# Taking the first three weight pairs of unit 0 in two chunks of 128 tokens, with a new stored order

## The chip, the cores and the metric

The kernel runs on one core of a Trainium2 chip. The metric is device microseconds of one execution. Five engines of the core work side by side, each through its own queue in order: TensorE (PE) with its weight loads (PEld), VectorE (DVE), ScalarE (ACT), GpSimd (POOL), and SyncE (SP), which issues all DMAs here.

## What is computed

A gated linear attention (complex decays, 4 x 8 heads of 48, 768 tokens) whose output goes through a feed-forward layer of 384 x 2048 x 384. All is float32; the weights w_in and w_out come in as 64-bit floats. Cut to what matters:

```python
def _attn_ref(q, k, v, a_re, a_im):
    mag = np.sqrt(a_re * a_re + a_im * a_im)
    scale = np.minimum(mag, 0.999) / (mag + 1e-06)
    a_re_n, a_im_n = (a_re * scale, a_im * scale)
    ...
    for t in range(S):
        ar, ai = (a_re_n[:, :, t, :, None], a_im_n[:, :, t, :, None])
        new_re = ar * S_re - ai * S_im
        new_im = ar * S_im + ai * S_re
        kv = np.einsum('bhd,bhe->bhde', k[:, :, t], v[:, :, t])
        S_re, S_im = (new_re + kv, new_im)
        y[:, :, t] = np.einsum('bhd,bhde->bhe', q[:, :, t], S_re)
    return y

def _moe_ref(x, w_in, w_out):
    h = x @ w_in
    g = h * (1.0 / (1.0 + np.exp(-1.702 * h)))
    return g @ w_out
```

## The kernel before

The 3072 tokens are 12 units of 256 (`T`), three to a batch; a unit is two chunks of 128 (`L`). For each unit the kernel does three things.

`prepare` turns the decays of a unit into magnitudes and angles: squares, logarithms, exponentials and an arctangent on ACT, sums and scans along time on DVE, then cosines and sines, and q and k are scaled and rotated (`rot0`, `rot1`). The small correction of the reference (the 1e-6) is two activations in stage `logc`: an exponential, then a logarithm. ACT must load another function table whenever it goes between logarithms, trigonometry and the Silu of the feed-forward layer (line 837). `remap` then copies the rotated q and k from tile `qr` or `qk` into tile `qkh` by five DMAs each. Unit 0 alone is prepared in its two chunks, so that chunk 0 is ready first.

`attend` works chunk by chunk on PE: scores (line 499, named P below), a masked copy `pm` on DVE, transposed keys (line 555, K) with a copy `kt`, the state (line 549, Z), and the mix of both (line 524) into `x_ps`. An x copy on ACT (line 534) puts the 128 columns of a chunk into tile `x`.

`moe` runs the feed-forward layer for a block of units: units 0 and 1 alone, then two at a time. It goes through 8 weight pairs `A0`..`A7`, `U0`..`U7` (`NP`). A pair has two halves `f`; each half has an H piece (line 605: three matmuls by an A tile into `h_ps`), a Silu on ACT (line 614 for units 0 and 1) and an O piece (line 638: three matmuls by a U tile, added up in `o_ps`). Blocks 0 and 1 take the weights whole as float32; all later blocks take each product as three terms, of high and low halves. Before block 0 can use a pair, `convert` makes it from the raw 64-bit words: two integer operations and an add on DVE (lines 297, 301, 304), one activation on ACT (line 300), in buffers that are loaded again once they are free. Thirteen matmuls by the identity (`WARM`, line 446) stand ahead of the attention of unit 0 and write nothing that is used.

At the end, `decide` sees whether the data are in the range that this way of computing needs. For this `prepare` and `extent` (line 692) reduce the decays; the last `LATE` units do it where the decays lie already, the others are loaded again for it.

The order of all this isn't found by a scheduler at run time. Each step is recorded with its engine and what it reads and writes (`Plan.add`), and a stored table, `ORDER`, says in which order the steps are written out; `OTHER` names the steps that go to their second engine (ACT or DVE). Each engine runs its steps in that order and waits for others where data ask for it. The two lines that the order hangs on:

```python
    order = plan.order()
    ...
            if o[5] not in (None, cur):
                nc.scalar.preload_act_table_set(o[5])
```

Of the kernel before, what the change touches and what calls it, by code (L numbers as in the profile page):

```python
# [23 lines left out]
P = 128  # L24
# [21 lines left out]
A_MIN = 1e-20  # L46
LOG_MAX = math.log(0.999)
LIFT = 14.0
LATE = 3
# [20 lines left out]
class Plan:  # L70
# [90 lines left out]
def attention_moe(ctx: ExitStack, tc: tile.TileContext, qk_in, v, a_in, w_in, w_out, qn, kn, vn, an, bn, out):  # L161
# [7 lines left out]

    ident = sb.tile([P, P], F32, name="ident")  # L170
    mask = sb.tile([P, NQ, P], F32, name="mask")
    small = sb.tile([P, 4 + 2 * NR], F32, name="small")
    ones, b_tiny, b_hpi, good = (small[:, n : n + 1] for n in range(4))
    crs = [small[:, 4 + n * NR : 4 + (n + 1) * NR] for n in range(2)]
    n_a, n_w = (NU + 1) * NR, 2 * NP * WC // CK
# [836 lines left out]
```

## Time and profile before

| | us |
|---|---|
| median of 3 runs | 561.31 (560.44 to 562.53) |
| the profiled execution | 560.85 |
| its span, first to last instruction | 559.1 |
| PE busy in the span | 532.4 |
| DVE busy | 406.7 |
| ACT busy | 354.3, of which 94.9 in 74 table loads |
| first attention matmul, first MoE matmul | 25.36, 38.52 |

The span is what the rows below are counted in, from its start. A busy time is the union of an engine's instructions; ends of matmuls are modelled, so the step from one start to the next says more than a duration. The first column of a row of a timeline is the start.

### The profile page before, as it was taken

Reading aid. Unit: us, or ns where it says so; the run is one execution under the profiler, and the core shown is the slowest. Engines: PE = TensorE matmul, PEld = TensorE weight load, DVE = VectorE, ACT = ScalarE, POOL = GpSimd, SP = SyncE. Lnnn points to the kernel's source line nnn. Section 1 sums busy time; section 2 is a strip of 40 time slices with the busy share of each in tenths; the row PEclk is TensorE's granted clock in tenths of the full one; section 3 lists DMA queues with packets and bytes.
Section 4 is the critical chain, followed back from the end, with each engine's and each line's share of the span. In section 5 each row is a group of like instructions: output and inputs, shape, how many; then the busy total and the mean of one; then the engine's idle time right before and its main releaser. Section 6 shows DMA issues by size and latency. Waiting matters only on the chain.

```text
span 559.1 us, 14720 instructions
## 1 busy us (share of the span) xinstructions
PE 532.4 (95%) x6236; PEld 442.7 (79%) x6236; DVE 406.7 (73%) x733; ACT 354.3 (63%) x500; POOL 28.7 (5%) x86
## 2 busy tenths in 40 slices
PE   0599999999999999999999999999999999999996
PEld 0478888888888888888888888887888888888884
DVE  7999999999998898978958856686665444422132
ACT  8999999998997788688494746536362122122222
POOL 4300010101000000000000000000000000000000
PEclk9999999999999999999999999999999999999999
DMA  8679977683758677486556456538225331001101
GB/s 338 201 270 349 252 241 151 191 199 90 212 121 232 143 181 173 135 219 143 182 134 130 131 118 146 175 108 164 72 84 162 86 73 52 2 9 31 55 1 59
DMA packets 32341, 81.24 MB, mean 145 GB/s; under 512 B 4368, under 2 KB 8464, under 8 KB 32272
## 3 DMA queue, kind: packets, MB, share of 16 engines
q1 hardware_dynamic: 32272, 80.27, 52.9%
q8 instruction: 49, 0.80, 0.6%
q14 instruction: 20, 0.16, 0.1%
HBM read 56.62 MB, written 4.72 MB: 110 GB/s over the span
## 4 chain that ended last, share of the span: by engine, by line
PE 89%; ACT 4%; DVE 4%; issue 1%; DMA 1%; POOL 0%; DVEq 0%; ACTq 0%
PE o_ps L638 35%; PE h_ps L605 35%; PE x_ps L524 7%; PE p_ps L499 5%; PE kz_ps L555 4%; PE kz_ps L549 3%; DVE qk L277 1%; ACT L837 1%; ACT valA L300 1%; DVE qr L277 1%; DMA ri<-in_a_dram 1%; DVE valA L304 0%; DVE s L277 0%; DVE s L419 0%; ACT s L375 0%
## 5 line engine op out<-in xcount | busy, mean ns | idle before, releaser
L618 ACT ACTIVATE g<-h_ps 128x512 f32<-128x512 f32 x80 | 46.8, 595 | 100.2 <-PE h_ps L605 85.7
L837 ACT ACT_TABLE_LOAD x74 | 94.9, 1283 | 2.1 <-PEq L1000 0.8
L638 PE MATMUL o_ps<-gh,hiU 128*128 128x512 f32 x240 | 95.8, 399 | 0.0
L605 PE MATMUL h_ps<-xhi,hiA 128*128 128x512 f32 x240 | 95.4, 397 | 0.1
L638 PE MATMUL o_ps<-gl,hiU 128*128 128x512 f32 x240 | 93.8, 391 | 0.0
L605 PE MATMUL h_ps<-xhi,loA 128*128 128x512 f32 x240 | 93.7, 390 | 0.0
L638 PE MATMUL o_ps<-gh,loU 128*128 128x512 f32 x240 | 93.5, 390 | 0.0
L605 PE MATMUL h_ps<-xlo,hiA 128*128 128x512 f32 x240 | 93.5, 390 | 0.0
L624 DVE TENSOR_TENSOR gl<-g,gh 128x512 fp32r<-128x512 f32 x80 | 54.7, 688 | 47.5 <-ACT gh L621 45.6
L638 PEld LDWEIGHTS o_ps<-gl,hiU 128*128 128x128 f32 x240 | 45.0, 188 | 10.1 <-DVE gl L624 0.4
L605 PEld LDWEIGHTS h_ps<-xhi,loA 128*128 128x128 f32 x240 | 45.1, 188 | 9.6
L605 PEld LDWEIGHTS h_ps<-xlo,hiA 128*128 128x128 f32 x240 | 45.1, 188 | 9.0 <-issue 0.3
L638 PEld LDWEIGHTS o_ps<-gh,hiU 128*128 128x128 f32 x240 | 45.1, 188 | 9.0 <-issue 0.2
L605 PEld LDWEIGHTS h_ps<-xhi,hiA 128*128 128x128 f32 x240 | 45.1, 188 | 8.9 <-ACT g L618 0.2
L638 PEld LDWEIGHTS o_ps<-gh,loU 128*128 128x128 f32 x240 | 45.2, 188 | 8.6
L672 DVE TENSOR_REDUCE fit<-raw_w 128x1 f32<-128x256 f32 x96 | 36.6, 413 | 17.2 <-DMA raw_w<-in_w_out_dram 12.9
L638 PE MATMUL o_ps<-g,valU 128*128 128x256 f32 x192 | 46.2, 384 | 0.1
L277 DVE TENSOR_TENSOR qk<-qk,s 128x768 f32<-128x768 f32 (+1 forms) x52 | 45.6, 889 | 0.3
L605 PE MATMUL h_ps<-x,valA 128*128 128x256 f32 x192 | 45.3, 383 | 0.0
L621 ACT ACTIVATE gh<-g 128x512 fp32r<-128x512 f32 x40 | 25.0, 627 | 24.8 <-PE o_ps L638 24.1
L605 PEld LDWEIGHTS h_ps<-x,valA 128*128 128x128 f32 x192 | 35.7, 190 | 5.2 <-ACT g L614 0.4
L638 PEld LDWEIGHTS o_ps<-g,valU 128*128 128x128 f32 x192 | 35.5, 190 | 5.5 <-ACT g L614 0.5
(96 smaller groups left out, 824.9 us busy)
## 6 DMA issues: line engine op xcount, KB each, us to landing
v<-in_v_dram SPq DMA_DIRECT2D x24, 416.0 KB, 4.5
ri<-in_a_dram SPq DMA_DIRECT2D x11, 768.0 KB, 5.4
qk<-in_qk_dram SPq DMA_DIRECT2D x11, 768.0 KB, 5.7
qkh<-qr SPq DMA_DIRECT2D x22, 288.6 KB, 6.0
qkh<-qk SPq DMA_DIRECT2D x22, 288.6 KB, 5.9
raw<-in_w_in_dram SPq DMA_DIRECT2D x8, 768.0 KB, 6.1
raw<-in_w_out_dram SPq DMA_DIRECT2D x8, 768.0 KB, 6.6
raw_w<-in_w_in_dram SPq DMA_DIRECT2D x24, 256.0 KB, 2.9
```

The source lines that it names most:

```text
L277: add(en, t, rank, lambda: e.tensor_tensor(out=out, in0=a, in1=b, op=alu), **kw)
L499: mm(p_ps[to : to + QL, j, lo:L], lhsT=at(h, 1, c)[:, lo : lo + QL], rhs=at(h, 0, c)[:, lo:L], start=True, stop=True)
L524: mm(x_ps[32 * j : 32 * j + 32, r, :], lhsT=lt, rhs=rt, start=n == 0, stop=n == len(steps) - 1)
L549: mm(z_ps[a:b, j * VP + lo : j * VP + lo + D], lhsT=kt[0][:, j, a:b], rhs=vt[:, h * VP + lo : h * VP + lo + D], start=True, stop=True)
L555: nc.tensor.transpose(k_ps[:, j, :], at(4 * hh + 2 * e + j, 1, c)[0:KD], ident[0:KD, 0:KD])
L605: mm(h_ps[hb][:, hs], lhsT=ww[:, r * T + f * P : r * T + (f + 1) * P], rhs=x[:, r, :], start=r + k == 0, stop=r == NR - 1 and k == len(ter ...
L618: add("ACT", a_t(N) - 0.15, rk(i + f / 2), lambda hb=hb, hs=hs: act(out=g32[hb][:, hs], in_=h_ps[hb][:, hs], func=AF.Silu, scale=SLOPE), r ...
L621: one = ("ACT", a_t(N) - 0.1, lambda hb=hb, hs=hs: act(out=high.g(hb)[:, hs], in_=g32[hb][:, hs], func=AF.Copy))
L624: add("DVE", d_t(N), rk(i + f / 2), lambda hb=hb, hs=hs: dve.tensor_tensor(out=glo[hb][:, hs], in0=g32[hb][:, hs], in1=high.g(hb)[:, hs].b ...
L638: mm(o_ps[m][:, 0:N], lhsT=y[:, f * DM + m * P : f * DM + (m + 1) * P], rhs=x[:, hs], start=i == 0 and f == 0 and k == 0, stop=i == NP - 1 ...
L672: add("DVE", d_t(CK), rk + 2, lambda x=x, op=op: dve.tensor_reduce(out=f_w[:, x, n : n + 1], in_=weights.looked_at()[:, :, 1], op=op, axis ...
L837: nc.scalar.preload_act_table_set(o[5])
```

## The change

Block 0 gets a list of steps in place of the loop over pairs: pairs 0, 1 and 2 (`EARLY = 3`) on chunk 0, the same three on chunk 1, then pairs 3 to 7 on all 256 columns. An H piece of a chunk reads that chunk's x copy alone; its matmuls have 128 columns. Besides:

- Stage `logc` is one exponential with a bias of log 1e-6 in place of an exponential and a logarithm.
- The first load of the decays, of chunk 0, is two DMAs, real parts first.
- The absolute value on DVE is a bitwise operation on integers.
- The range of the decays is judged by their real parts alone, against 0.125; `LATE` is 6, and `extent` loads real parts only, in two pieces a unit.
- In the last pair of the last block the three groups of half 0 stand ahead of those of half 1, and the last of three outputs is evicted and stored in two halves.
- `ORDER` and `OTHER` are new throughout.

In the whole program PE gets 36 matmuls more (72 of 128 columns for 36 of 256), ACT has 50 table loads in place of 79 and DVE 20 reductions fewer, among others. The counts include the fallback path that isn't run.

```diff
+EPS = 1e-6
+R_MIN = 0.125
-LATE = 3
+LATE = 6
+EARLY = 3
...
-        add("SP", z, rk("load"), lambda: dma(out=ri[:, cols], in_=a_in[u, :, cols]), w=ks("re", "im"))
+        for x in range(2) if u == i == 0 else (2,):
+            part = slice(cols.start + x % 2 * C, cols.stop if x else cols.start + C)
+            add("SP", z * (0.5 if x < 2 else 1), rk("load"), lambda part=part: dma(out=ri[:, part], in_=a_in[u, :, part]),
+                w=[k for n, kind in enumerate(("re", "im")) if x in (n, 2) for k in ks(kind)])
...
-        add("ACT", a_t(C) - 0.1, rk("logc"), lambda: act(out=c, in_=m, func=AF.Exp, scale=-0.5), r=k_mag, w=k_rec, tab=LOGS, grp=u or None)
-        add("ACT", a_t(C), rk("logc"), lambda: act(out=c, in_=c, func=AF.Ln, scale=1e-6, bias=ones), w=k_rec, tab=LOGS, grp=u or None)
+        add("ACT", a_t(C) - 0.1, rk("logc"), lambda: act(out=c, in_=m, func=AF.Exp, scale=-0.5, bias=b_eps), r=k_mag, w=k_rec, tab=LOGS, grp=u or None)
...
-        two = ("DVE", d_t(C), lambda: dve.scalar_tensor_tensor(out=cs, in0=t, scalar=-1.0, in1=t, op0=ALU.mult, op1=ALU.max))
+        two = ("DVE", w_t(C), lambda: dve.tensor_scalar(
+            out=cs.bitcast(I32), in0=t.bitcast(I32), scalar1=0x7FFFFFFF, scalar2=None, op0=ALU.bitwise_and,
+        ))
...
-        for i in range(NP):
-            def at(f, i=i):
-                k = (2 * i + f) % 2 if len(units) == 2 else 2 * f + i % 2
-                return k * N // (2 * T), slice(k * N % (2 * T), k * N % (2 * T) + N), f"{k * N // T}"
+        steps = [(i, 0, N) for i in range(NP)]
+        if n == 0:
+            steps = [(i, c * L, L) for c in range(2) for i in range(EARLY)] + steps[EARLY:]
+        for t, (i, c0, M) in enumerate(steps):
+            def at(f, i=i, t=t, M=M):
+                k = (2 * i + f) % 2 if len(units) == 2 else 2 * f + t % 2
+                return k * N // (2 * T), slice(k * N % (2 * T), k * N % (2 * T) + M), f"{k * N // T}"
+
+            nm = f"{n}c" if M < N else f"{n}"
+            xk = [f"x{y}{b}.{c}" for y in ("h" if whole else "hl") for c in range(c0 // L, (c0 + M) // L)]
...
-                        terms = [(weights.whole("A", i), high.x0(n))]
+                        terms = [(weights.whole("A", i), high.x0(n)[:, :, c0 : c0 + M])]
...
-                parts = [((0, 1), (m,)) for m in range(NR)]
+                parts = [((0,), tuple(range(NR)))] + [((1,), (m,)) for m in range(NR)]
...
+        pieces = [(m, 0, N) for m in range(NR)]
+        if final:
+            pieces[-1:] = [(NR - 1, 0, N // 2), (NR - 1, N // 2, N)]
```

Where the work of unit 0 stands on PE. In the kernel before, the last warm-up and the last K turn of chunk 1 stand ahead of the first H pieces (`x` is the tile of both chunks, `valA` an A tile, `h_ps` and `o_ps` the sums):

```order
L446 MATMUL h_ps_105<-qk,ident 128x256
L555 MATMUL kz_ps<-ident,qkh_75 128x112 x2
L605 MATMUL h_ps_106<-x_407,valA_157 128x256 x3
L605 MATMUL h_ps_105<-x_407,valA_293 128x256 x3
L605 MATMUL h_ps_106<-x_407,valA_293 128x256 x3
L605 MATMUL h_ps_105<-x_407,valA_157 128x256 x3
L638 MATMUL o_ps_107<-g_497,valU_181 128x256
```

In the changed kernel (its line 614 is line 605 of before, 503 is 499, 559 is 555), from the second H piece on:

```order
L614 MATMUL h_ps_105<-x_377,valA_215 128x128 x3
L503 MATMUL p_ps<-qkh_75 32x128 x4
L503 MATMUL p_ps<-qkh_75 32x96 x4
L503 MATMUL p_ps<-qkh_75 32x64 x4
L503 MATMUL p_ps<-qkh_75 32x32 x4
L559 MATMUL kz_ps<-ident,qkh_75 128x112 x2
L614 MATMUL h_ps_105<-x_377,valA_236 128x128 x3
L614 MATMUL h_ps_106<-x_377,valA_236 128x128 x3
L503 MATMUL p_ps<-qkh_75 32x128 x4
```

H pieces of 128 columns have moved between the scores of chunk 1; before, all scores came first.

On ACT, the kernel before has the two x copies (line 534) of unit 0 five rows apart, then a table load and the first Silu (line 614):

```order
L534 ACTIVATE x_407<-x_ps 128x3x128
L374 ACTIVATE s_81<-s_81 128x3x256
L558 ACTIVATE kt_97<-kz_ps 128x224
L837 ACT_TABLE_LOAD
L391 ACTIVATE s_81<-s_81 128x3x256
L534 ACTIVATE x_407<-x_ps 128x3x128
L300 ACTIVATE valA_467<-raw_72 128x768
L837 ACT_TABLE_LOAD
L614 ACTIVATE g_488<-h_ps_106 128x256
```

The changed kernel, from its first x copy (line 538) on; 623 is the Silu, 844 the table load, 303 a weight, and the others are steps of unit 1:

```order
L538 ACTIVATE x_377<-x_ps 128x3x128
L562 ACTIVATE kt_97<-kz_ps 128x224
L303 ACTIVATE valU_374<-raw_73 128x768
L428 ACTIVATE s_81<-s_85 128x3x256
L404 ACTIVATE s_80<-s_84 128x3x256
L405 ACTIVATE s_84<-s_84 128x771
L844 ACT_TABLE_LOAD
L623 ACTIVATE g_463<-h_ps_105 128x128
```

Its second x copy stands 19 rows behind the first:

```order
L844 ACT_TABLE_LOAD
L379 ACTIVATE s_81<-ri,small 128x3x256
L538 ACTIVATE x_377<-x_ps 128x3x128
L380 ACTIVATE s_81<-s_81 128x3x256
L381 ACTIVATE s_83<-s_83,small 128x3x256
L562 ACTIVATE kt_97<-kz_ps 128x224
L386 ACTIVATE s_84<-s_83,small 128x3x256
L844 ACT_TABLE_LOAD
L623 ACTIVATE g_463<-h_ps_105 128x128
```

Silus of chunk 0 now stand between the two x copies, and so do steps of unit 1 and 2 that came later before.

## Rows read from the trace of the kernel before

**Rows 1.** Page, part 1: busy us, share of the span, instructions

```profile
PE 532.4 (95%) x6236; PEld 442.7 (79%) x6236; DVE 406.7 (73%) x733; ACT 354.3 (63%) x500; POOL 28.7 (5%) x86
```

**Rows 2.** Busy time by stretch: stretch, length, busy us of each engine, granted clock, DMA

```profile
25.36:38.52 13.16, 11.47 (x309) 8.39 (x308) 12.47 (x21) 12.51 (x19) 0.14 (x2) 1.00 0.68 220
38.52:540.00 501.48, 501.30 (x5851) 418.78 (x5850) 369.41 (x654) 314.67 (x440) 17.46 (x53) 1.00 0.53 140
```

**Rows 3.** Timeline of PE, 25 to 50 us: start, us, line, operation, form, count

```profile
25.36 0.36 PE L555 MATMUL kz_ps<-ident,qkh 112*128 112x112 f32 x2
25.65 0.76 PE L499 MATMUL p_ps<-qkh 128*32 128x128 f32 x32
...
38.52 5.47 PE L605 MATMUL h_ps<-x,valA 128*128 128x256 f32 x24
43.83 1.46 PE L638 MATMUL o_ps<-g,valU 128*128 128x256 f32 x6
45.12 1.46 PE L605 MATMUL h_ps<-x,valA 128*128 128x256 f32 x6
...
49.30 0.53 PE L549 MATMUL kz_ps<-v,kt 128*32 128x48 f32 x32
```

**Rows 4.** The chain that ended last: a whole mix of a chunk

```profile
82.51 1.89 PE x_ps L524 x64
```

**Rows 5.** Groups at 25.4 us, then weight loads at 38.5 us: busy, mean ns

```profile
L555 PE MATMUL kz_ps<-ident,qkh 112*128 112x112 f32 x2 | 0.4, 260 | 0.0
...
L605 PEld LDWEIGHTS h_ps<-x,valA 128*128 128x128 f32 x1 | 0.2, 186 | 0.0
...
38.47 0.30 PEld L605 LDWEIGHTS h_ps<-x,valA 128*128 128x128 f32 x2
```

**Rows 6.** Timeline of ACT, 4 to 42 us

```profile
3.97 0.52 ACT L260 ACTIVATE s<-ri 128x384 f32<-128x384 f32 x1 [1.89 <-DMA ri<-in_a_dram]
4.40 0.60 ACT L373 ACTIVATE s<-ri,small 128x384 f32<-128x384 f32 x1
4.90 1.33 ACT L260 ACTIVATE s<-ri 128x384 f32<-128x384 f32 x3
...
10.02 1.28 ACT L837 ACT_TABLE_LOAD   x1
...
33.04 0.35 ACT L558 ACTIVATE kt<-kz_ps 128x224 f32<-128x224 f32 x1
33.27 0.94 ACT L384 ACTIVATE s<-s,small 128x768 f32<-128x768 f32 x1
34.10 0.49 ACT L534 ACTIVATE x<-x_ps 128x384 f32<-128x384 f32 x1
34.47 0.85 ACT L374 ACTIVATE s<-s 128x768 f32<-128x768 f32 x1
...
37.94 0.48 ACT L534 ACTIVATE x<-x_ps 128x384 f32<-128x384 f32 x1
...
40.70 0.38 ACT L614 ACTIVATE g<-h_ps 128x256 f32<-128x256 f32 x1
40.98 1.08 ACT L300 ACTIVATE valU<-raw 128x768 uint16<-128x768 uint32 x1
```

**Rows 7.** Timeline of SyncE's queue: first and last issues of chunk 1's remap

```profile
24.31 1.17 SPq L461 DMA_DIRECT2D qkh<-qr  x2
...
29.44 2.09 SPq L464 DMA_DIRECT2D qkh<-qk  x2
```

**Rows 8.** Timeline of the tail: weight loads, then SyncE's queue

```profile
550.80 0.19 PEld L638 LDWEIGHTS o_ps<-gl,hiU 128*128 128x128 f32 x1 [0.45 <-DVE gl L624]
...
551.97 3.11 SPq L659 DMA_DIRECT2D out_dram<-o  x3
```

**Rows 9.** Busy time by stretch, warm-up matmuls alone: PE, PEld, granted clock, DMA

```profile
19.93:22.98 3.05, 3.04 (x7) 2.48 (x8) 1.00 0.66 131
22.98:25.36 2.38, 2.38 (x12) 1.90 (x10) 1.00 0.43 108
```

More of the change, by code (lines that the diff above doesn't have):

```diff
@@ L171, in attention_moe @@
     mask = sb.tile([P, NQ, P], F32, name="mask")
[L172 to L174 removed]
+    small = sb.tile([P, 5 + 2 * NR], F32, name="small")
+    ones, b_tiny, b_hpi, good, b_eps = (small[:, n : n + 1] for n in range(5))
+    crs = [small[:, 5 + n * NR : 5 + (n + 1) * NR] for n in range(2)]
     n_a, n_w = (NU + 1) * NR, 2 * NP * WC // CK
[L176 to L178 removed]
+    n_e, n_r = NU - LATE, NU + LATE
+    fit = sb.tile([P, n_a + n_r + 2 * n_w], F32, name="fit")
     f_a = fit[:, 0:n_a].rearrange("p (u r) -> p u r", r=NR)
@@ L577, in moe @@
         final = n == len(BLOCKS) - 1
-        xk = [f"x{y}{b}.{c}" for y in ("h" if whole else "hl") for c in range(2 * len(units))]
         both_halves = "v" if whole else "hl"
@@ L650, in moe @@
         spent = [f"x{y}{b}.{c}" for y in "hl" for c in range(4)]
         to = out[:, u0 * T : u0 * T + N].rearrange("(m p) t -> p m t", p=P)
-        for m in range(NR):
-            one = ("ACT", a_t(N) - 0.12, lambda m=m: act(out=high.o(n)[:, m, 0:N], in_=o_ps[m][:, 0:N], func=AF.Copy, scale=1.0 / SLOPE))
-            two = ("DVE", d_t(N), lambda m=m: dve.tensor_scalar(
-                out=high.o(n)[:, m, 0:N], in0=o_ps[m][:, 0:N], scalar1=1.0 / SLOPE, scalar2=None, op0=ALU.mult
-            ))
-            either("A" if final and m == NR - 1 else "D", one, two, rk(NP + 0.1), r=[f"o{m}"], w=[f"ob{m}"] + ([] if final else spent))
@@ L658, in moe @@
-        for ms in (((0,), (1,), (2,)) if final else ((0, 1, 2),)):
-            add("SP", len(ms) * N * P * 4 / 410e3, rk(NP + 0.1), lambda ms=ms: dma(
-                out=to[:, ms[0] : ms[-1] + 1, :], in_=high.o(n)[:, ms[0] : ms[-1] + 1, 0:N]
-            ), r=[f"ob{m}" for m in ms] + ([] if final else spent))
+        pieces = [(m, 0, N) for m in range(NR)]
+        if final:
+            pieces[-1:] = [(NR - 1, 0, N // 2), (NR - 1, N // 2, N)]
+        for q, (m, lo, hi) in enumerate(pieces):
+            one = ("ACT", a_t(hi - lo) - 0.12, lambda m=m, lo=lo, hi=hi: act(
+                out=high.o(n)[:, m, lo:hi], in_=o_ps[m][:, lo:hi], func=AF.Copy, scale=1.0 / SLOPE
+            ))
+            two = ("DVE", d_t(hi - lo), lambda m=m, lo=lo, hi=hi: dve.tensor_scalar(
+                out=high.o(n)[:, m, lo:hi], in0=o_ps[m][:, lo:hi], scalar1=1.0 / SLOPE, scalar2=None, op0=ALU.mult
+            ))
+            either("A" if final and m == NR - 1 else "D", one, two, rk(NP + 0.1), r=[f"o{m}"], w=[f"ob{q}"] + ([] if final else spent))
+            if final:
+                add("SP", (hi - lo) * P * 4 / 410e3, rk(NP + 0.1), lambda m=m, lo=lo, hi=hi: dma(
+                    out=to[:, m, lo:hi], in_=high.o(n)[:, m, lo:hi]
+                ), r=[f"ob{q}"])
@@ L663, in inspect @@
+        if not final:
+            add("SP", NR * N * P * 4 / 410e3, rk(NP + 0.1), lambda: dma(out=to, in_=high.o(n)[:, :, 0:N]),
+                r=[f"ob{m}" for m in range(NR)] + spent)
     def inspect(n):
@@ L700, in judge @@
             for a, lim, op in (
-                (fit[:, 0:n_a], A_MIN, ALU.is_ge),
+                (fit[:, 0:n_a], A_MIN, ALU.is_ge), (f_r, R_MIN, ALU.is_ge),
                 (f_w[:, 0, :], W_MIN, ALU.is_ge), (f_w[:, 1, :], W_MAX, ALU.is_lt),
```

132 lines of the change are left out of this document (60 added, 72 removed), and 14 rows, old and new, of the table OTHER.

## The prediction

> **What bounds the kernel now.** I read the totals first: TensorE (PE) is busy 532.4 of 559.1 us, VectorE (DVE) 406.7, ScalarE (ACT) 354.3 [rows 1]. Such shares are means, so the table by stage comes next [rows 2]: from the first feed-forward (MoE) matmul at 38.52 [rows 3] to 540, PE is busy 501.30 of 501.48 us, while DVE and ACT have 132 and 187 us free in the same stretch. So what ACT or DVE save after 38.52 buys nothing by itself. Three things alone can move the end: how early PE becomes full, how much work PE is given, and the tail behind its last matmul. Before 38.52 it is the other way round: in the 13.16 us from PE's first attention matmul on, ACT is busy 12.51 and DVE 12.47 [rows 2]. Those two set when unit 0 is ready and when weights are converted.
>
> **Part 1, the split of the first three pairs.** Before, the first H piece needs both chunks of unit 0: their x copies stand at 34.10 and 37.94 on ACT [rows 6], the first H follows at 38.52. After, H on chunk 0 needs only the first x copy. So I need the times of both x copies in the new order, and ACT, which is full, gives them. I count the step from start to start, the duration less about 0.1 of overlap (three squares of 384 columns in 1.33: 0.41 each): 0.41 for 384 columns, 0.50 with a bias tile, 0.75 and 0.83 for 768 columns, 0.25 for a kt copy, 0.37 for an x copy, 0.96 for a weight half; a table load costs 1.28 and the 0.1, since the one ahead of it drains [rows 6].
> ACT's list from the first square to the first x copy. Before: 17 x 0.41 + 8 x 0.50 + 6 loads x 1.38 + 4 x 0.75 + 3 x 0.83 + 4 x 0.96 + 3 x 0.25 = 29.3. From 3.97 that gives 33.3, and it came at 34.10: 0.8 went in waits. After: 18 x 0.41 + 8 x 0.50 + 4 loads x 1.38 + 4 x 0.75 + 3 x 0.83 + 5 x 0.96 + 3 x 0.25 = 27.9. The start moves from 3.97 to 3.97 - 0.5 at best, since ACT waits there for the first load of a [rows 6] and that load is now cut in two; I take 3.45. With 0.8 of waits again, and 0.4 for abs and the turns, which now wait for DVE inside one group, the first x copy starts at 32.5 and the first H at 33.0.
> From there to the second x copy ACT has one x copy, 2 kt copies, 2 weight halves, 5 x 0.75, 2 x 0.83, 2 table loads and 6 Silus of 128 columns at 0.28 at most, what one of 256 takes (40.70 to 40.98) [rows 6]: 12.6 at most, 11.8 if half the columns take half the time. I take 12: the second x copy at 44.5, and chunk 1's H pieces from 45.0 on. That is 7 us later than before, since ACT now does work of unit 1 in between.
> What PE has for the 12 us from 33.0 to 45.0: a whole piece takes 1.29 us (43.83 to 45.12) [rows 3], a half one 0.65 if columns are the price. Six H and five O pieces on chunk 0 stand there in its order, 7.2 us; with two groups of scores at 0.7, a mix of 1.9 [rows 4], two turns of K at 0.3 and two Z at 0.5 [rows 3] that is 12.1. So PE is full there, or nearly. Chunk 1's remap doesn't decide it: its ten DMA issues take 7.2 us of SyncE's queue (24.31 to 31.53) [rows 7] and now wait behind a weight load and DVE's later rotations, so the scores come at about 35 in place of 32.7, but four H pieces cover that.
> Compare at 45.0. Scores and mixes of both chunks are done in either order. Before, MoE has run from 38.52: 6.5 us. After, 7.2, and one Z of 0.5 that before does only at 49.30 [rows 3]. PE is ahead by **1.2**.
> Then it gives some back. Behind the second x copy ACT has 0.37 + 0.75 + 0.83 + 0.25 + 0.83 + 1.38 = 4.4 us, a table load last, until its next Silu; chunk 1's first g is there at about 49.2. PE has four half H pieces, one K and one O piece until then, 3.5 us, and waits **0.7**. Lead at 60 us: 0.5.
>
> **Part 2, the price of narrow matmuls.** 36 whole matmuls become 72 half ones; each is two instructions in the trace, so 72 more instructions and weight loads. The streamed columns are the same, but a load must now fit under half a stream. The trace has no 128-column matmul over the full array. The nearest row is a pair of K turns with 112 columns: 0.36 us for two that take 0.26 each, so the second starts 0.10 behind the first with a full-height load between, about what its columns cost [rows 5]. The other end: two loads of the full array end 0.30 after the first began, one takes 0.19, so they follow at 0.11 [rows 5]; with none of it hidden, 144 instructions x 0.11 = +15.8. I take the K row, +0.2, and keep the other end as a rival; a gain is excluded, as no column is saved. Besides, PE enters MoE work from attention work 73 times in place of 63, and six of the ten come from K turns. A piece behind such a change shows 1.46 where one behind MoE steps 1.29 [rows 3]: between 0 and 10 x 0.17. I take 0.3.
>
> **Part 3, edits with one answer.** One exponential for two activations, 29 fewer table loads, fewer reduces, abs as a bitwise operation, larger extents and LATE: all on ACT, DVE or SyncE behind a PE that is full [rows 2], and before that already in the lists above. Gain and price 0. The cover is PE's own work; a stretch without it would be worth up to 1.38 a load, but none shows.
>
> **Part 4, the tail.** Before, PE's last pair waits 0.45 for its low half, at 550.80 [rows 8]; the f = 0 groups now stand ahead of all f = 1 groups, so half a pair covers it, and what of 0.45 wasn't hidden goes: -0.2. Then one eviction and one DMA become two halves each. Three issues took 3.11 us, the last until 555.08 [rows 8]; a fourth makes SyncE end up to 0.3 later, with half the bytes left to move. I take 0, bounds -0.4 and +0.3.
>
> **Sum.** -0.5 (lead, with the +0.2 in the 0.65) + 0.3 (entries) - 0.2 (tail) = -0.4 us. The profiled execution took 560.85 (span 559.1), so it would take 560.4; the median of the runs is 561.31, and there I expect **560.9**. About 0.5%, 2.8 us, is what a measurement of this kernel can tell from no change.
>
> **The rivals.**
> (a) Faster: ACT waits less. The 1.2 us ahead of the first x copy go, so does the 0.7 behind the second, the entries cost nothing, and the tail is at its best: 560.9 - 1.2 - 0.7 - 0.3 - 0.2 = 558.5. For it: unit 0's trigonometric work stands in two groups in the new order and is chopped less by table loads. Against: DVE serves the same list and had 0.7 us free in 13 [rows 2].
> (b) Slower: weight loads don't hide under 128 columns. Place: 33 to 59 us; price: 144 x (step - 0.11). It decides for slower from a step of about 0.14 on. With nothing hidden it is +15.8, less some 1.5 of PE's waits that it fills: 575; at a step of 0.15 it is 565. Against: the K row.
> (c) The clock. From 19.93 on, seven warm-up instructions took 3.05 us, the next eleven 2.38 [rows 9]: 0.43 against 0.22 each, the pace of 1.2 and of 2.4 GHz, though the granted clock reads 1.00 in both rows. Ahead of the slow ones PE had done nothing. Before, four more warm-ups stand among unit 0's attention; after, two, right ahead of the first H, and PE has some 4 us of work from 24 to 33. If the clock falls there, it costs 3.05 - 7 x 0.22 = 1.5 us to get back: 562.4.
> The Trainium skill ("TensorE: Matmul & The Clock Gate", Part 1) says that half rate is the default, that activity lifts it and idleness brings it back; by that rule this rival comes true and the sum is 562.4. The trace agrees that work behind an idle stretch starts at half pace; no row of it shows a fall later on.
> (d) Slower: weights come too late. DVE's list puts unit 1's and 2's preparation between the adds of pairs 3 to 7, and it has next to nothing free. A piece that waits holds PE's queue for up to a piece, 1.29; three of them: 564.8.
>
> **How the numbers follow.** Forecast (559.5 to 562) 0.56; (a) 0.20; (b) 0.09; (c) 0.10; (d) 0.05. Faster by over 0.5%: (a), 0.20. Within: forecast and (c), 0.66. Slower: (b) and (d), 0.14. The range leaves out (b), (d) and the far part of (a): 557.8 to 563.5.
>
> **What would show it.** Right: first 128-column H at about 33, second x copy on ACT at 44 to 45, a wait of PE for a Silu just behind it, a step of 0.11 in the narrow matmuls, PE full from 50 on. Wrong: that step at 0.14 or more (b) or at 0.22 (c), PE waiting for DVE's weight adds between 55 and 80 (d), the second x copy at 42 (a).

## The result: 0.6% slower, and where the time went

| | kernel before | kernel after |
|---|---|---|
| median, us | 561.04 (560.44 to 562.53, 6 runs) | 564.41 (563.64 to 566.04, 6 runs) |
| ratio | | 1.0059, 95% interval 1.0048 to 1.0069 |
| profiled execution, and its span, us | 560.85, 559.1 | 564.28, 562.6 |
| start of the last MoE matmul | 553.70 | 555.41 |
| from there to the end | 5.45 | 7.17 |

Forecast was 560.9 in a range of 557.8 to 563.5; the kernel took 564.4. The profiled executions show two halves of the loss: PE starts its last MoE matmul 1.7 us later, and what follows it takes 1.7 us longer.

The page of the kernel after, its totals, answers to [rows 1]:

```profile
PE 534.3 (95%) x6308; PEld 448.1 (80%) x6308; DVE 398.1 (71%) x721; ACT 305.1 (54%) x458; POOL 33.2 (6%) x86
```

ACT has 49 us less to do and DVE 9 us less, and the kernel is slower. The table by stretch, the answer to [rows 2] (stretch, length, busy us of PE, PEld, DVE, ACT, POOL, granted clock, DMA share, GB/s), shows why that bought nothing and what is new:

```profile
24.26:28.00 3.74, 1.46 (x37) 1.00 (x35) 3.04 (x7) 3.74 (x8) 1.33 (x2) 0.99 0.96 327
28.00:30.00 2.00, 1.43 (x32) 1.43 (x32) 1.85 (x3) 1.98 (x2) 0.31 (x2) 0.50 1.03 406
30.00:32.00 2.00, 2.00 (x34) 1.46 (x35) 1.75 (x3) 1.11 (x2) 0.00 (x0) 0.50 0.75 154
32.00:34.00 2.00, 1.46 (x45) 1.23 (x38) 1.34 (x3) 0.64 (x2) 0.00 (x0) 0.50 0.30 66
34.00:36.00 2.00, 1.62 (x7) 1.10 (x6) 1.45 (x3) 2.00 (x4) 0.43 (x2) 0.82 0.60 152
36.00:45.00 9.00, 8.95 (x152) 8.32 (x153) 8.94 (x16) 8.75 (x15) 0.44 (x4) 1.00 0.88 313
300.00:540.00 240.00, 240.00 (x2620) 198.34 (x2619) 127.30 (x250) 82.86 (x129) 3.71 (x13) 1.00 0.36 91
```

From 36 us on PE is full, as before. From 24.26 to 28 it was busy for 1.46 of 3.74 us, and then the granted clock reads 0.50, the 1.2 GHz level, until 34.7. The timeline of PE (start, us, line, operation, form, count, wait ahead of it and its releaser), the answer to [rows 3]:

```profile
26.25 0.41 PE L559 MATMUL kz_ps<-ident,qkh 112*128 112x112 f32 x2 [0.94 <-ACT kt L562]
28.57 1.59 PE L503 MATMUL p_ps<-qkh 128*32 128x128 f32 x32 [1.92 <-DVE pm L507]
30.10 0.64 PE L559 MATMUL kz_ps<-ident,qkh 112*128 112x112 f32 x2
30.66 1.94 PE L528 MATMUL x_ps<-pm,v 128*32 128x128 f32 x32
32.37 0.87 PE L553 MATMUL kz_ps<-v,kt 128*32 128x48 f32 x32
...
35.89 0.94 PE L614 MATMUL h_ps<-x,valA 128*128 128x128 f32 x6 [0.38 <-ACT x L538]
36.76 0.54 PE L553 MATMUL kz_ps<-v,kt 128*32 128x48 f32 x32
...
41.59 0.94 PE L647 MATMUL o_ps<-g,valU 128*128 128x128 f32 x6
42.36 0.83 PE L614 MATMUL h_ps<-x,valA 128*128 128x128 f32 x6
...
45.34 0.42 PE L528 MATMUL x_ps<-pm,v 128*32 128x128 f32 x8
```

Scores that took 0.76 at full clock [rows 3] take 1.59 at 28.57. The first H piece stands at 35.89, not at 33.0. The wait ahead of the scores at 28.57 is for a mask, which stands on DVE behind four rotations of chunk 1. DVE's timeline:

```profile
25.08 1.16 DVE L280 TENSOR_TENSOR qr<-qk,s 128x384 f32<-128x384 f32 x2
26.77 1.15 DVE L280 TENSOR_TENSOR qk<-qk,s 128x384 f32<-128x384 f32 x2 [0.53 <-DVE qr L280]
27.84 0.68 DVE L507 TENSOR_TENSOR pm<-p_ps,mask 128x512 f32<-128x512 f32 x1
```

ACT then waits 2.25 us for PE, where [rows 6] show no such wait. Its timeline after, with both x copies (L538) and the first Silu (L623):

```profile
30.18 0.94 ACT L381 ACTIVATE s<-s,small 128x768 f32<-128x768 f32 x1
33.36 0.36 ACT L562 ACTIVATE kt<-kz_ps 128x224 f32<-128x224 f32 x1 [2.25 <-PE kz_ps L553]
...
35.38 0.47 ACT L538 ACTIVATE x<-x_ps 128x384 f32<-128x384 f32 x1
...
41.00 0.28 ACT L623 ACTIVATE g<-h_ps 128x128 f32<-128x128 f32 x1
...
47.93 0.47 ACT L538 ACTIVATE x<-x_ps 128x384 f32<-128x384 f32 x1
```

SyncE's queue, the answer to [rows 7]: chunk 1's remap is issued from 28.25 to 35.63, four us later than before, and the loads behind it, the values of chunk 1 (v) among them, go out only then:

```profile
28.25 1.16 SPq L465 DMA_DIRECT2D qkh<-qk  x2
...
34.41 1.22 SPq L468 DMA_DIRECT2D qkh<-qr  x2
35.73 0.53 SPq L373 DMA_DIRECT2D ri<-in_a_dram  x1
36.37 0.65 SPq L409 DMA_DIRECT2D qk<-in_qk_dram  x1
37.06 1.14 SPq L495 DMA_DIRECT2D v<-in_v_dram  x2
```

The tail, first the last MoE matmul of the kernel after, then its last store alone (DMA queues with packets, MB and share; then the issue with KB and us to landing):

```profile
555.41 0.39 PE L647 MATMUL o_ps<-gl,hiU 128*128 128x512 f32 x1
```

```profile
q14 instruction: 4, 0.03, 2.8%
q8 instruction: 1, 0.02, 2.0%
out_dram<-o SPq DMA_DIRECT2D x1, 128.0 KB, 4.2
```

And the same two of the kernel before:

```profile
553.70 0.39 PE L638 MATMUL o_ps<-gl,hiU 128*128 128x512 f32 x1
```

```profile
out_dram<-o SPq DMA_DIRECT2D x1, 256.0 KB, 2.5
```

Half the bytes took 4.2 us where the whole had taken 2.5. In that stretch the queues marked "instruction" move 0.05 MB in the kernel after and 0.03 MB in the kernel before.

### The profile page after: what moved, and what is told of

Same layout as the page of the kernel before. It is cut to its first block, busy times and chain, and to the rows that moved or that the text cites. A ratio compares the mean times of both kernels' runs of the same rounds, so it can differ in the third digit from the quotient of the medians.

```text
span 562.6 us, 14807 instructions
## 1 busy us (share of the span) xinstructions
PE 534.3 (95%) x6308; PEld 448.1 (80%) x6308; DVE 398.1 (71%) x721; ACT 305.1 (54%) x458; POOL 33.2 (6%) x86
## 4 chain that ended last, share of the span: by engine, by line
PE 93%; DVE 4%; ACT 1%; issue 1%; DMA 0%; POOL 0%; DVEq 0%; ACTq 0%
PE o_ps L647 37%; PE h_ps L614 36%; PE x_ps L528 7%; PE p_ps L503 5%; PE kz_ps L559 4%; PE kz_ps L553 3%; DVE qk L280 1%; DVE s L398 1%; DVE valA L307 0%; DVE s L280 0%; DMA ri<-in_a_dram 0%; DVE qr L280 0%; DVE s L421 0%; DVE s L431 0%; DVE raw L304 0%
## 5 line engine op out<-in xcount | busy, mean ns | idle before, releaser
L627 ACT ACTIVATE g<-h_ps 128x512 f32<-128x512 f32 x80 | 46.5, 597 | 126.6 <-PE h_ps L614 100.1
L631 DVE CAST gh<-g 128x512 fp32r<-128x512 f32 x41 | 17.3, 423 | 44.6 <-PE o_ps L647 39.9
L614 PE MATMUL h_ps<-x,valA 128*128 128x256 f32 (+1 forms) x228 | 46.6, 350 | 0.4 <-ACT x L538 0.4
L647 PE MATMUL o_ps<-g,valU 128*128 128x256 f32 (+1 forms) x228 | 46.7, 351 | 0.0
L630 ACT ACTIVATE gh<-g 128x512 fp32r<-128x512 f32 x39 | 24.1, 627 | 40.6 <-PE o_ps L647 40.4
L614 PEld LDWEIGHTS h_ps<-x,valA 128*128 128x128 f32 x228 | 37.6, 190 | 4.8 <-ACT x L538 0.8
```

The source lines that it names most:

```text
L614: mm(h_ps[hb][:, hs], lhsT=ww[:, r * T + f * P : r * T + (f + 1) * P], rhs=x[:, r, :], start=r + k == 0, stop=r == NR - 1 and k == len(ter ...
L627: add("ACT", a_t(N) - 0.15, rk(i + f / 2), lambda hb=hb, hs=hs: act(out=g32[hb][:, hs], in_=h_ps[hb][:, hs], func=AF.Silu, scale=SLOPE), r ...
L630: one = ("ACT", a_t(N) - 0.1, lambda hb=hb, hs=hs: act(out=high.g(hb)[:, hs], in_=g32[hb][:, hs], func=AF.Copy))
L631: two = ("DVE", d_t(N, 2), lambda hb=hb, hs=hs: dve.tensor_copy(out=high.g(hb)[:, hs], in_=g32[hb][:, hs]))
L647: mm(o_ps[m][:, c0 : c0 + M], lhsT=y[:, f * DM + m * P : f * DM + (m + 1) * P], rhs=x[:, hs], start=i == 0 and f == 0 and k == 0 and c0 == ...
```

## How the start is compared

A time of one event says little when orders differ, so for each kernel I counted the matmuls that start after a given moment, each at its full-clock step (0.227 us for 512 columns, 0.216 for 256, 0.112 for 128, attention's by its rows at full clock, dummies 0), and subtracted the sum for the kernel before. The result is how far PE is behind the kernel before, in us of its own work:

| kernel | 36 us | 45 us | 48 us | 60 us | 100 us | last MoE matmul |
|---|---|---|---|---|---|---|
| after | 3.3 | 3.0 | 3.2 | 2.9 | 3.0 | 555.41 |
| e1_clock | 2.2 | 2.8 | 3.4 | 3.1 | 3.9 | 556.20 |
| e3_mask | 2.4 | 2.8 | 3.4 | 3.1 | 3.5 | 555.74 |
| e4_xcopy | 1.3 | 2.6 | 2.6 | 2.3 | 2.6 | 554.84 |
| e5_value | 3.4 | 3.4 | 3.5 | 3.3 | 3.5 | 555.97 |
| e6_value_clock | 2.1 | 2.7 | 2.8 | 2.7 | 3.9 | 556.52 |
| e10_clock_value | 1.8 | 1.5 | 2.8 | 2.9 | 3.5 | 555.96 |
| e12_layers | 1.9 | 1.4 | 1.3 | 1.8 | 1.7 | 554.43 |
| e14_first | 1.4 | 3.7 | 4.9 | 4.6 | 5.0 | 557.29 |

The kernel after is 2.9 us behind at 60 us, and 1.2 of it comes back until the last matmul.

Two things limit this table. How attention's matmuls are weighed moves the column at 36 us by up to 0.7, the others by up to 0.5. And each row is one execution: PE's first matmul stands at 17.8 us in most kernels, but at 18.1 in e1, 18.3 in e5, 18.6 in e14 and 18.8 in e3, ahead of anything that these edits move; in e3 and e14 DVE waits 0.9 and 0.8 us there, at 9 to 11 us, for the first weights and the first q and k. That much in these four rows is chance.

## Experiments on the tail

In the diffs below all edits are made to the kernel after.

**e2_tail**: the last third of the output in one piece again.

```
+            none = final and q == NR - 1
+            lo = 0 if final else lo
...
-            one = ("ACT", ..., lambda ...: act(
+            one = ("ACT", ..., lambda ...: none or act(
...
-                add("SP", ..., lambda ...: dma(
+                add("SP", ..., lambda ...: none or dma(
```

The piece of the first half does nothing, that of the second takes all columns.

> The changed kernel with the last 128 rows of the output evicted by one instruction and stored by one DMA, as before the change, in place of two of each; the order of the matmuls stays. Theory A, the split end costs: from the start of the last MoE matmul to the end of the program it takes 5.4 us as before the change, in place of 7.2, and the time falls by 1.8, to about 562.6 us. Theory B, the longer end has another source (code loading or the order of the last matmuls): it stays at 6.8 us or more, and the time at 564 us or more.

562.73 us, ratio to before 1.0032 (1.0020 to 1.0044): 1.5 us less than the kernel after by the ratios. From the last MoE matmul (555.23) to the end it takes 5.7 us. Theory A holds. (Its start has the order of the kernel after, yet in its profiled execution the clock read 0.50 only from 29.7 to 33.1 us; the comparison by the tails, 7.2 against 5.7, is free of that.) The last store alone:

```profile
out_dram<-o SPq DMA_DIRECT2D x1, 256.0 KB, 2.8
```

**e11_store**: two evictions, one store that waits for both.

```
+            none = final and q == NR - 1
+            lo = 0 if final else lo
...
-                add("SP", ..., lambda ...: dma(
+                add("SP", ..., lambda ...: none or dma(
...
-                ), r=[f"ob{q}"])
+                ), r=[f"ob{q}", f"ob{max(q - 1, 0)}"])
```

> The changed kernel with the last 128 rows of the output still evicted in two halves of 256 columns, but stored by one DMA that waits for both. Theory A, the fourth store is what costs: its 128 KB set out last, in rows of 1 KB, and still move when the program's last branch has the closing code loaded by the same DMA engines (in the changed kernel the last store's completions spread over 2.2 us). With one store of 2 KB rows the end stands 5.4 to 5.8 us after the last MoE matmul, the time at 562.8 us. Theory B, the second eviction is what costs: 6.7 us or more, the time at 564 us.

563.31 us, ratio 1.0037 (1.0022 to 1.0051), tail 5.7 us: theory A; the second eviction costs nothing that shows in the tail, the fourth store does. Over all kernels profiled with four stores (after, e1, e3, e4, e5, e6, e10) the tail is 6.7 to 7.2 us; with three (before, e2, e7, e8, e9, e11, e12, e13, e14) 5.1 to 5.7, but for 6.3 in e12. Why the fourth store lands late is open. Its rows of 1 KB alone aren't the reason: the half store ahead of it has them too and landed in 2.0 us. Nor are the 0.05 MB on the queues marked "instruction" enough by themselves, since e2 moves as much there and its last store landed in 2.8 us; no run took them away.

## Experiments on the start

In these diffs a pair in MOVES puts the operation named first right behind the second in the stored order: M is a mask multiplication, P scores, K key transposes, kt their copy, Z the state's matmuls, X a copy of x, W a warm-up, H0c0 an H step on chunk 0, v values, add the end of a weight's conversion, rot and remap the rotations and the remap, edge a copy of the decays' edge, each with unit, chunk and half; f is a load of raw weights; a bare number is a place in the stored order.

**e1_clock**: six dummy matmuls into PE's idle stretches.

```
+    def spin(n):
+        for _ in range(n):
+            mm(h_ps[0][:, 0:T], lhsT=ident, rhs=mask[:, 0:2, :], start=True, stop=True)
 def scores(...):
+    if u == c == hh == 0: spin(2)
 def turn(...):
+    if u == c == hh == 0 and e == 1: spin(4)
```

> The changed kernel with six more dummy matmuls (identity by mask, 128 x 256, into the hidden bank that the warm-ups use): two behind the first scores of unit 0 and four behind the second pair of transposes. They stand where TensorE of the changed kernel idled (25.3 to 26.2 and 26.7 to 28.6 us), and nothing is computed from them. Theory A, the clock: the granted clock stays at 1.00 between 26 and 36 us, the second scores, the mix and the first state take 0.8, 1.0 and 0.45 us in place of 1.6, 1.9 and 0.9, the first matmul of the MoE comes at about 34.2 in place of 35.9 us, and the time falls by about 1.7, from 564.4 to some 562.7 us. Theory B, the order on VectorE and ScalarE sets the start: the clock is back at 1.00 but the first matmul of the MoE stays at 35.3 or later, and the time at 564 us or more.

564.91 us, ratio 1.0081 (1.0056 to 1.0106): no gain, though the clock reads 1.00 from 24 to 48 us, the first H comes at 34.70, and PE is only 1.7 us behind at 44 (kernel after: 3.0). Neither theory as put: A's mechanism came, its gain didn't. PE's timeline shows where it went:

```profile
45.69 0.43 PE L534 MATMUL x_ps<-pm,v 128*32 128x128 f32 x8 [1.63 <-DMA v<-in_v_dram]
```

In the kernel after the values of chunk 1, asked for at 37.06, took 7.7 us and landed at 44.8 (not at 45.4, as the expectation of e5 has it); the mix began at 45.34. The slow clock had hidden a load that was nearly as late.

**e3_mask** and **e4_xcopy**: the order on DVE, and on ACT, alone.

```
+MOVES = (("M0.0.0", "P0.0.0"), ("P0.0.1", "K0.0.0.1"), ("M0.0.1", "rot0.1.11"))
```

> The changed kernel with the two mask multiplications of unit 0's first chunk moved up in VectorE's order: the first ahead of the two rotations of chunk 1 that write qk, the second right behind these; nothing else moves. Theory A, VectorE's order let TensorE idle, and the clock fell for it: the second scores start at about 27.0 in place of 28.6 us, the second mask is done at 28.8 in place of 30.9, the mix ends at 30.0 (32.6), the first matmul of the MoE comes at 33 to 34 us, the time falls by 1.5 to 2.5, to about 562.4 us. Theory B, the clock alone: it falls all the same at about 28 us, the mix ends at 31.5, the first matmul of the MoE comes at 34.8, and the time is 563.4 us. Theory C, ScalarE's order sets the start: the first copy of x stays later than 34.5 us and the time at 564 us.

```
+MOVES = (("X0.0", "Z0.0.0"), ("W11", "K0.0.0.1"), ("W12", "W11"), ("H0c0.0", "X0.0"))
```

> The changed kernel with unit 0's first copy of x moved up in ScalarE's order, ahead of the copy of transposed keys, one logarithm-table step and one weight conversion that it stood behind, and with the first H step and the last two warm-ups moved up on TensorE to go with it. Theory A, ScalarE's order held the start up: the copy runs at 32.7 in place of 35.4 us, the first matmul of the MoE comes at about 33.5 in place of 35.9, and the time falls by 1.5 to 2.4, to 562 to 563 us. Theory B, the first Silu at 41.0 us (a table load behind a list of ScalarE work) sets when the first O step may start: the first matmul of the MoE comes early, TensorE waits for the Silu instead, and the time falls by less than 0.5, to about 564 us.

e3 took 564.12 us, ratio 1.0055 (1.0042 to 1.0069): the same as the kernel after. The second mask was done at 29.7, the mix at 31.1, the clock stayed up, and at 46 us PE was as far behind as in e1. Less the 0.9 us by which this execution began late, these are about A's 28.8 and 30.0, and the first H (34.90) stands at 34.0: A's mechanism came, its gain didn't, since PE waits 1.5 us for the values as in e1 (the mix begins at 45.72). The x copy at 34.38, near C's 34.5, holds the same late start. e4 took 563.79 us, 1.0057 (1.0041 to 1.0073): theory B. The first H came at 31.93, four us earlier than in the kernel after, and the first O at 40.96, only 0.6 earlier, since the first Silu still stands at 40.37. In between PE ran dry:

```profile
31.90:36.00 4.10, 2.65 (x52) 2.17 (x52) 2.97 (x6) 3.09 (x5) 0.50 (x2) 1.00 0.45 110
36.00:41.00 5.00, 3.79 (x76) 3.19 (x73) 5.00 (x10) 4.74 (x7) 0.42 (x2) 1.00 0.83 285
```

**e5_value** and **e6_value_clock**: the values early, without and with the dummies of e1.

```
+MOVES = (("v0.1", "f7"),)
```

> The changed kernel with one DMA moved: the values of unit 0's chunk 1 (416 KB) are asked for at about 25 us, right behind a weight load, in place of 37 us, behind the eight or so DMAs of the two remaps and two other loads. In the changed kernel they landed at 45.4 us, and the mix of chunk 1 began at 45.3. Theory A, two causes in a row: the slow clock keeps TensorE busy until the values land, so the earlier values alone give little: the mix at 44.5 to 45.0, time down by 0 to 0.5, to 564.0 to 564.4 us. Theory B, the values alone set the second half of the start: the mix at 43.5, time down by 1.3 or more, to 563.1 us.

> The changed kernel with the earlier values of the run e5_value and the six dummy matmuls of the run e1_clock together. Theory A, two causes in a row, each hidden by the other (the dummies alone gave nothing, since TensorE then waited 1.6 us for the values): together they take 1.2 to 1.7 us off, to about 563.0 us, the first matmul of the MoE at 34.7 and the mix of chunk 1 at 44.1 us, with no wait for the values. Theory B, something else holds the mix of chunk 1 at 45 us (the state's decay or the masks): the time stays at 564.4 us.

e5: 564.50 us, 1.0079 (1.0052 to 1.0107), no gain, as theory A had it, though the mix came at 45.85 and not at 44.5 to 45.0; this execution began 0.5 us late, with the clock at 0.50 from 28.3 to 35.1. e6: 565.18 us, 1.0075 (1.0058 to 1.0092): no gain either, against A. PE no longer waits for the values, but the 416 KB now go ahead of chunk 1's remap:

```profile
PE p_ps L514 <- DMA qkh<-qr: 0.9, 2, 0.7
```

**e10_clock_value**: the dummies, and the values between the remap and the loads for unit 1, where they don't hold the remap up.

```
+MOVES = (("v0.1", 133),)
```

> The changed kernel with the six dummy matmuls of e1_clock and with the values of chunk 1 asked for between the remaps of chunk 1 and the loads for unit 1 (at about 36 us, ahead of 1.5 MB), where they don't hold up the remap as in e6_value_clock. Theory A, the slow clock costs 1.2 us once neither values nor remap take its place: values landed by 39 us, first matmul of the MoE at 34.7, no wait of TensorE at the mix of chunk 1, mix at 44.0, time 562.9 to 563.3 us. Theory B, the clock costs nothing by itself: 564.2 us or more, as in e1_clock.

566.52 us, 1.0085 (1.0064 to 1.0106). Up to 46 us the trace does what theory A said: 1.5 us behind, no wait at the mix, which begins at 43.75. Then PE gives 1.4 us back to the next wait (line waited for: us, times, longest):

```profile
PE o_ps L666 <- DVE valU L318: 1.4, 1, 1.4
```

It waits for the third pair's output weights. Their conversion stands on DVE behind work of unit 1 that needs the load of qk, which the values now go ahead of:

```profile
45.05 0.96 DVE L291 TENSOR_TENSOR qk<-qk,s 128x768 f32<-128x768 f32 x1 [2.32 <-DMA qk<-in_qk_dram]
```

The profiled execution took 564.93 us; four of the six took 566.3 to 567.6, and no trace shows what these lost.

**e12_layers**: values and addition put right, the clock held by four of the kernel's own warm-ups, the single last store of e2.

```
+MOVES = (("v0.1", 133), ("addU2", "M0.1.1"),
+         ("W9", "P0.0.0"), ("W10", "W9"), ("W11", "K0.0.0.1"), ("W12", "W11"))
```

> The changed kernel with four of its thirteen warm-ups put elsewhere in TensorE's order (two behind the first scores, two behind the second pair of transposes, no instruction more than before), the values of chunk 1 between the remaps and the loads for unit 1 as in e10_clock_value, the addition that ends the conversion of the third pair's output weights moved up on VectorE to right behind the second mask of chunk 1, and the undivided last store of e2_tail. In e10_clock_value TensorE was 1.45 us behind the kernel before up to 46 us and then lost 1.4 more to a wait for that addition. Theory A, layers: with the clock at 1.00 and neither values nor that addition late, TensorE stays 1.2 to 1.6 us behind from 45 to 100 us, and the time is 1.2 us under that of e2_tail, 561.4 to 561.8 us, the same as before the change within 0.2%. Theory B, a further wait takes the 1.4 us again: 562.5 us or more.

In the profiled execution the waits behind 36 us are gone, and PE stays 1.3 to 1.8 us behind to 100 us, as theory A said; what is left stands ahead of the first H:

```profile
PE h_ps L625 <- ACT x L549: 1.7, 1, 1.7
PE p_ps L514 <- DVE pm L518: 1.0, 1, 1.0
PE kz_ps L570 <- ACT kt L573: 0.8, 2, 0.5
```

But the time is 563.01 us, ratio 1.0036 (1.0024 to 1.0049): that of e2_tail, not 1.2 us less. In the profiled executions the last MoE matmul starts 0.8 us earlier than in e2 (554.43 against 555.23), and 0.6 of that is lost behind it, where the last store takes 3.4 us to land and not 2.8:

```profile
out_dram<-o SPq DMA_DIRECT2D x1, 256.0 KB, 3.4
```

**e8_three**, **e7_all** and **e9_start**: bundles. e8 joins the edits of e5, e4 and e2; e7 adds those of e3 and the second copy of x right behind its mix; e9 puts the whole start in another order, with e2's store:

```
+MOVES = (("edge0.0", "rot0.1.01"), ("remap0.1.0", "edge0.0"), ("v0.1", "remap0.1.1"), (157, 136),
+         ("X0.0", "Z0.0.0"), ("W11", "K0.0.0.1"), ("W12", "W11"), ("H0c0.0", "X0.0"),
+         ("H0c0.1", "K0.0.1.1"), ("P0.1.0", "H0c0.1"), ("M0.1.0", 143), (166, "Z0.0.1"), (183, 166),
+         ("K0.1.0.0", 183), ("P0.1.1", "K0.1.0.0"), ("M0.1.1", "P0.1.1"), ("mix0.1.0", "M0.1.1"),
+         ("mix0.1.1", "mix0.1.0"), ("mix0.1.2", "mix0.1.1"), ("X0.1", 180))
```

> The changed kernel with the earlier values of e5_value, the earlier copy of x with its warm-ups of e4_xcopy, and the undivided last store of e2_tail. If the causes add up: the tail gives 1.7, the start 2.0 to 2.5 (first matmul of the MoE at 32, mix of chunk 1 at 43.5): 560.2 to 560.8 us, no slower than before the change. Rival: a next wait takes the start's gain (the remap of chunk 1, the second weight pair, the first Silu at 40 us): 562 us.

> The run e8_three's kernel with the earlier masks of e3_mask as well, and with unit 0's second copy of x right behind its mix in ScalarE's order, ahead of a logarithm table load that it stood behind. If the order on VectorE and ScalarE is what is left: first matmul of the MoE at 31, second copy of x at 45.0 in place of 47.9, the time 0.5 to 1.0 below e8_three, at about 559.5 to 560 us. Rival: ScalarE now waits for the mix and hands the delay to the Silus and the table work behind it: equal to e8_three or up to 0.7 above it.

> The changed kernel with the undivided last store of e2_tail and with the whole start put in another order: both rows of chunk 1's remap swapped so that qr, ready first, goes first; the values of chunk 1 right behind the remaps and ahead of the loads for unit 1; the first copy of x, the first two H steps and the warm-ups early as in e4_xcopy; VectorE's conversion of the second pair's input weights, its masks of chunk 1 and its update of the state moved up; the mix of chunk 1 ahead of the O pieces. Theory A, TensorE loses its time before about 41 us to a row of waits, each hidden behind the one before it (first copy of x, remap, masks, values), and only all of them together give it back: TensorE full from 32 us on, mix of chunk 1 done by 42, second copy of x by 43 to 44, and the time 2 to 2.5 us under that of e2_tail, at 560.2 to 560.8 us. Theory B, the first Silu at 40 us and the six half H pieces that it holds back set the start whatever stands before it: TensorE waits for the Silu from 38 to 40.5, and the time is at 562 us or more.

562.80 us (1.0060, 1.0035 to 1.0085), 565.45 us (1.0084, 1.0071 to 1.0097) and 565.92 us (1.0070, 1.0051 to 1.0089): no gain over e2 each time, as the rivals had it, but e7 stands 2.7 us above e8, where its rival allowed 0.7. In e8 PE waits 1.4 us for the remap behind the values; in e7 1.5 for the first copy of x, 1.7 for the remap, and 1.4 for a key copy at 52.3. Right behind the wait for the remap the clock fell in both, to 0.50 from 37.6 to 41.0 us in e8 and from 37.1 to 40.5 in e7; by half of that stretch it cost about 1.7 us of PE's work. In e8 the same twelve matmuls ahead of it and in it:

```profile
31.95 1.60 PE L621 MATMUL h_ps<-x,valA 128*128 128x128 f32 x12 [0.27 <-ACT x L545]
...
38.21 2.91 PE L621 MATMUL h_ps<-x,valA 128*128 128x128 f32 x12
```

In e9 PE is 0.7 us behind at 38 and 5.1 at 45: the state's copy, which the next transposes need, had to stand behind scans on DVE, and PE was idle until 40.6; and the clock read 0.50 from 39.7 to 46.5, so that PE's work from 40.6 to 45 gave up about 2.2 us more. Theory B's wait for the Silu isn't there. So in all three bundles the clock took a price of its own, later than in the kernel after. The longest wait of e9:

```profile
PE kz_ps L570 <- DVE st L583: 2.5, 1, 2.5
```

**e14_first** and **e13_silu**: what holds the rest of e12.

```
+MOVES += (("X0.0", "Z0.0.0"), (149, "X0.0"), (137, 134), (148, 137), (155, 148),
+          (157, 136), (139, 157), (153, 139), (165, 153), (169, 165))
```

> The kernel of e12_layers with the first copy of x ahead of the key copy it stood behind, the first H step around the key transposes, and VectorE's conversion of the second pair's input weights moved into a gap at 33 us, so that the second H step can follow at once. Theory A, the Silu holds the rest: the first matmul of the MoE comes at 32.0 instead of 34.35 us and TensorE is 0.3 to 0.7 us behind the kernel before at 36, but it runs out of pieces ahead of the first Silu (39 us) and is 1.3 us behind or more at 42; the time is that of e12_layers within 0.4, about 563 us. Theory B, the waits ahead of the first H are the rest: 0.7 us behind or less from 36 to 60 us, the time 0.7 to 1.0 us under e12_layers, about 562 us.

```
+MOVES += (("X0.1", 202), (159, "X0.1"), (163, 159), (167, 163),
+          (199, "addU2"), ("addA4", 199), (194, 163), (201, 167))
```

> The kernel of e14_first with the two exponentials for unit 1 moved on ScalarE from ahead of the first Silu to behind the second copy of x, where the same table is loaded anyway, with the work that needs them moved behind them, and with one weight conversion moved up into the gap that this leaves on VectorE. The first Silu comes at about 37 in place of 39.2 us. Theory A, the Silu holds the rest: TensorE is 0.7 us behind the kernel before or less at 45 and at 60 us, the time 0.7 to 1.2 us under e14_first, about 562 us. Theory B, something else holds it: the time is that of e14_first or above, unit 1 being ready later.

e14: 563.58 us, 1.0036 (1.0022 to 1.0050), the time of e12. PE is 1.4 us behind at 36 and 3.4 at 42, but the Silu is only 0.3 of it; remap and mask are more:

```profile
38.42 1.07 PE L514 MATMUL p_ps<-qkh 128*32 128x128 f32 x32 [0.92 <-DMA qkh<-qr]
...
40.91 1.06 PE L514 MATMUL p_ps<-qkh 128*32 128x128 f32 x32 [1.08 <-DVE pm L518]
...
42.32 0.94 PE L658 MATMUL o_ps<-g,valU 128*128 128x128 f32 x6 [0.34 <-ACT g L634]
```

So the time that A gave came for another reason, as far as this trace goes: it is of a long execution (564.42), which began 0.8 us late. e13: 570.41 us, 1.0151 (1.0132 to 1.0169). The first Silu came at 38.65, PE was 0.4 us behind at 38 and 3.4 at 45 (1.8 us of it one mask; the clock read 0.50 from 40.2 to 43.6), and then unit 1, whose exponentials had been put off, cost another 4.5, behind which the clock read 0.50 again, from 53.9 to 60.7; at 60 us PE is 10.1 behind:

```profile
PE kz_ps L570 <- ACT kt L573: 4.5, 1, 4.5
```

No kernel here beats the kernel before; the best of the edited ones, e2_tail, is 0.3% behind it.

## Why the prediction was wrong

**What bounds the kernel: right.** PE is full from 36 us on, 240.00 of 240 us between 300 and 540. The 49 us less on ACT bought nothing.

**Part 1, the time of the first x copy: the step that failed.** I summed ACT's list as if ACT alone set the time, with 0.8 + 0.4 us for waits: 32.5. It came at 35.38. ACT began at 3.26 (3.45 taken) and waited 0.73 for DVE and 2.25 for PE, 1.8 more than I had; the list itself took 1.2 more. The 2.25 us are one wait, at 31.1, for PE's Z, at the end of a chain that I had not followed: rotations of chunk 1 on DVE, mask, scores, mix and Z, the last three at half clock. With the clock held up (e1) the copy came at 34.18, so about 1.2 of the 2.9 us are the clock's, inside this chain. The list from the first x copy to the second was right: 12.55 us for 12. So the second copy came at 47.93 for 44.5, 3.4 late, 2.9 of it from the first.

PE's list behind the first H was short too. The nine groups of narrow matmuls from 35.89 to 49.0 take 8.3 us from start to start where I had 7.2 and 0.3 for entries: six take 0.67 behind MoE work (42.36 to 43.03) and 0.87 behind attention (35.89 to 36.76). Together: 2.9 + 0.8, and half a us that I can't place, turn the 1.2 us ahead at 45 into 3.0 behind. The 0.7 us wait behind the second x copy never came, since PE had its pieces still to do.

I also named four H pieces as cover for chunk 1's later remap. True in the kernel after (its scores follow a H piece without a wait), but I passed over what else stands in SyncE's queue behind that remap: the values of chunk 1 and two loads for unit 1. e1 shows that they were the next limit.

**Part 2, the narrow matmuls: right on the step, short on the entries.** 12 of them took 1.56 us from 39.03 on, 0.13 each with the entry; within a group the step is 0.112. The loads hide, rival (b) did not come.

**Part 3: nothing in the runs speaks against it.** ACT's 49 us less bought nothing, but no run tries one of these edits alone.

**Part 4, the tail: the other step that failed.** The wait of 0.45 is gone: the steps of the last pair are 0.227 throughout. But for the split store I took 0, at most +0.3, from the time of the issues alone ("with half the bytes left to move"). By the times of e2 and e11 it costs 1.2 to 1.5 us, by the tails of their profiles 1.5 (7.2 against 5.7): the store that sets out last took 4.2 us to land, more than the whole of before.

**Rival (c), the clock: it came; that it sets the time isn't shown.** Place and level were as written: 0.50 from about 28, behind a stretch of little work. By the rule of the Trainium skill ("TensorE: Matmul & The Clock Gate", Part 1) that idleness brings the half rate back, the trace agrees (0.50 in three of the stretches above), though PE wasn't idle throughout ahead of them. Its price, 1.5 us forecast, shows as 1.2 to 1.5 us of PE's lead up to 44 us (kernel after against e1 and e10). In three kernels that kept the clock up (e1, e6, e10) none of it reached the end: the values, the remap and the weights of the third pair stood right behind. The dummies may have a price of their own, too: from 60 to 100 us these three lose another 0.6 to 1.2 us and the kernel after 0.1, in e6 0.8 of it in a wait of PE at 80 us for which the profile names no releaser.

The single executions on record are a second test, since the mean granted clock differs within one kernel (0.992 in the profiled execution of the kernel after, with 0.50 from 27.9 to 34.7). In e12 four of twelve have 0.991 or 0.992, so its warm-ups didn't always hold the clock: these took 563.4 to 564.5 us, the other eight a median of 562.5. In e8 three with 0.994 or less took 564.3 to 568.1, four with 0.996 or more 562.4 to 562.8. In the kernel after and in e2 the execution with the highest clock is the longest (566.04 and 564.15). In the traces the clock fell behind waits of PE, so a longer wait can stand behind both the low clock and the time; no run parts the two.

**What stays open.** The split store accounts for 1.2 to 1.5 of the 3.4 us. The rest lies in the start, and there the runs show no single cause but a row of waits, each uncovered by removing the one ahead of it: clock, values, remap, weights, masks, Silu. With the clock, values and weights put right (e12), PE is 1.5 us less behind in the trace, and the runs show no gain over e2, or 0.4 us by medians, each against the kernel before, if only the eight executions of e12 with the higher clock are taken. So I can say which waits make up the late start, not that any one of them is worth its length in time.

## What to carry to other kernels

When an engine's list is summed to date an event, the sum is a lower bound: for each thing on the list that another engine delivers, date that too, and do the same for what stands in the DMA queue behind a step that moves. In a start where several chains run with little slack, the length of a wait is not what its removal gains; expect the next chain behind it at once. At the end of a program, count a store by when it lands, and not by its bytes. And a profile is one execution: before two are compared, see whether they agree ahead of the first thing that the edit moves; here they differed by up to 0.9 us.

## What the runs showed of the hardware

The granted clock fell to 0.50 though PE had done three pieces of work in the 3.7 us before (1.46 us busy from 24.26 to 28.00), and it stayed at 1.00 in e4, where PE was busy 2.65 of 4.10 us and then 3.79 of 5.00. With the same order in the start it read 0.50 from 27.9 to 34.7 us in the kernel after and from 29.7 to 33.1 in e2. The last store of the kernel after, 128 KB, took 4.2 us to land, with some 0.05 MB on the queues marked "instruction" in that stretch; the 128 KB issued just ahead of it took 2.0.
